# Scales of a two-part kernel: the mask to a power of two moves in front of the step across the partitions, and that step becomes a bfloat16 product instead of a float32 transpose

## The chip, the cores and the metric

The kernel runs on one core of one Trainium2 chip. The metric is the device time of one execution in microseconds. Three runs of the kernel before took 1719.19, 1721.06 and 1722.6 us; the median, 1721.06 us, is the time that a change is measured against. A separate, profiled execution gives the trace.

## The reference

Two independent results stand side by side in the output, 2048 x 2048 in float32.

```python
# A: attention with 32 heads of 32, each position sees itself and the 255 before it
qkv = (x @ wqkv).reshape(B, S, 3, H, Dh).transpose(2, 0, 3, 1, 4)      # S 2048, D 1024
scores = einsum("bhqd,bhkd->bhqk", q, k) * Dh ** -0.5, masked to 0 <= i - j < 256
a = (softmax(scores) @ v).reshape(B, S, D) @ wo
# B: Fourier mixing, real part, by matrices
re, im = einsum("bsd,ed->bse", x, dft_hid_re), einsum("bsd,ed->bse", x, dft_hid_im)
b = einsum("ts,bse->bte", dft_seq_re, re) - einsum("ts,bse->bte", dft_seq_im, im)
return concatenate([a, b], axis=-1)
```

## The kernel before

**Numbers.** Every large product is made from float16 halves. An operand is divided by a power of two s, its value is rounded to float16 (the hi part, on ScalarE), and what is left is rounded to float16 as well (the lo part, on VectorE). A product of two such operands is three float16 products: hi hi, hi lo, lo hi (`PASSES`). The pair of instructions is `split` (L123): an ACTIVATE at L126, then a SCALAR_TENSOR_TENSOR that goes through the helper `vec` and so stands under L120 in the profile.

**Scales.** The power of two of an operand comes from its largest absolute value. Reductions (`top`, or `u_top` on ScalarE) leave the largest of each partition in a tile named `top_...` of 128 x 1 float32 (`spread` joins the pieces). `scale_of` (L158) takes it across the partitions: TensorE transposes the tile, broadcast to 128 x 128, against a float32 identity (`ident`) into a PSUM tile `pt_...`; VectorE reduces that to one maximum on each partition, masks the mantissa away (`bitwise_and` with 0x7F800000, which leaves a power of two), bounds and multiplies it, and takes the reciprocal. 65 scales are made so: 16 for the blocks of the query and key weights (`w_scale`, results in `scw`, and for the input blocks in `vx`), 4 for the blocks of A's input, 2 for the value weights, 1 for the output weights, 8 for B's input (`xp`), 2 for the hidden Fourier matrices (`wd`), and 32 for the column blocks of the sequence Fourier matrices (`u_scale`, results in `sc_u`).

**The start.** Up to the seventh task of the list of projections (`head` and `strict` true) everything is in an order written by hand: `mm` chains each product behind the product before it on TensorE, and `vec` chains each VectorE operation behind the VectorE operation before it. The scale's TensorE step is part of that chain (L161 to L163). The first four projections, one for each of four blocks of query weights, are float32 products of unsplit operands (`d_mm`, tile `pq`, lines L726 to L731), with the scales between them (lines L883 to L918): largest values of weight block 0 and of input block 0, half of the first projection, scale of weight block 0, and so on. Their outputs leave through `qk_out` (tile `yq`, hi on ScalarE at L873, lo on VectorE). Input block 1 is split at L909 to L916, and the float16 projections follow.

**Later.** After the seventh task only TensorE's large products keep their written order. What stands on VectorE, ScalarE and around the scales' TensorE steps is placed by the framework's scheduler, which runs a timeline of its own over the program and gives each engine a fixed queue.

**The Fourier half** runs in four phases of 12 units: four units `x`, in which TensorE makes the hidden transform in blocks (seven products of half size each, `seven`), and eight units `c`, which multiply column blocks of a sequence matrix (`un_a`, `un_b`, `un_c`, split from `raw_u`) by the sums that the units `x` leave in `tsum`, a part of `reg`. The sums are written in `t_fill` (L822: hi on ScalarE at L824, lo on VectorE at L825), the last of them in `t_last`, while the first unit `c` begins: its second product (tile `p_b`) multiplies by a sum whose lo part is the last `reg<-y` of VectorE's fills. Attention of A is woven between the products of both parts (`tick`): scores `s` and `far`, probabilities, their transposed halves, and products `pv`.

Of the kernel before, what the change touches and what calls it, by code (L numbers as in the profile page):

```python
# [9 lines left out]
F32 = mybir.dt.float32  # L10
F32R = mybir.dt.float32r
F16 = mybir.dt.float16
BF16 = mybir.dt.bfloat16
U8 = mybir.dt.uint8
U32 = mybir.dt.uint32
AF = mybir.ActivationFunctionType
ALU = mybir.AluOpType
AX = mybir.AxisListType

P = 128  # L20
# [33 lines left out]
def fused_kernel(ctx: ExitStack, tc: tile.TileContext, xa, wqk, wv, wo, xb, wd, cs, out):  # L54
    nc = tc.nc
# [8 lines left out]
    const = ctx.enter_context(tc.tile_pool(name="const", bufs=1))  # L64
# [13 lines left out]
    tsum = reg1[:, :7 * 8 * CH].rearrange("p (s h k c) -> p s h k c", s=7, h=2, k=4)  # L78
    spare = reg1[:, 7 * 8 * CH:]

    ident = const.tile([P, P], F32, name="ident")
    make_identity(nc, ident)


    upper = const.tile([P, P], F32, name="upper")
# [13 lines left out]
    def bank(name):  # L99
        nbank[0] += 1  # L100
        return ps_m.tile([P, CH], F32, tag=f"m{nbank[0] % 3}", name=name)
# [7 lines left out]
    fixed = []  # L109

    def mm(*args, **kwargs):
        with tc.issue_after(fixed[0].ins) if fixed else nullcontext():
            fixed[:] = [nc.tensor.matmul(*args, **kwargs)]  # L113
        return fixed[0]
# [3 lines left out]
    def vec(f, *args, **kwargs):  # L118
        with tc.issue_after(latest[0].ins) if strict[0] and latest else nullcontext():
            latest[:] = [f(*args, **kwargs)]  # L120
        return latest[0]
# [12 lines left out]
    tops, head = {}, [True]  # L134
# [22 lines left out]

    def scale_of(key, v, s, down=2.0 ** -14):  # L158

        if head[0]:  # L160
            pt = ps_s.tile([P, CH], F32, tag="s", name=f"pt_{key}")[:, :P]  # L161
            with tc.issue_after(fixed[0].ins) if fixed else nullcontext():
                fixed[:] = [nc.tensor.transpose(pt, tops.pop(key).to_broadcast([P, P]), ident)]  # L163
        else:
            pt = (ps_v.tile([P, CH], F32, tag="pv", name=f"pt_{key}") if units_on else bank(f"pt_{key}"))[:, :P]
            nc.tensor.transpose(pt, tops.pop(key).to_broadcast([P, P]), ident)
        vec(nc.vector.tensor_reduce, v, pt, axis=AX.X, op=ALU.max)
        vec(nc.vector.tensor_scalar, v.bitcast(U32), v.bitcast(U32), 0x7F800000, None, op0=ALU.bitwise_and)
        vec(nc.vector.tensor_scalar, v, v, 2.0 ** -100, down, op0=ALU.max, op1=ALU.mult)
        vec(nc.vector.reciprocal, s, v)  # L170

# [245 lines left out]
    def w_scale(kd, g):  # L417
        v = vw[kd, g] = scw[:, "qk".index(kd), g]
        scale_of(f"w{kd}{g}", v[:, 0:1], v[:, 1:2])
# [26 lines left out]
    def x_scale(c):  # L446
        scale_of(f"x{c}", vx[:, 0, c:c + 1], vx[:, 1, c:c + 1])
# [22 lines left out]
    def wv_scale(vh):  # L470
        scale_of(f"wv{vh}", vwv[:, 0, vh:vh + 1], vwv[:, 1, vh:vh + 1])
# [398 lines left out]
    with tc.tile_pool(name="pa", bufs=2) as pa:  # L870
# [49 lines left out]
        for n, (kd, g, c) in enumerate(order):  # L920
# [12 lines left out]
            if kd == "v":  # L933
                t = c
# [9 lines left out]
                                                            op0=ALU.mult, op1=ALU.subtract)]  # L944
# [291 lines left out]
```

## Time and profile before

| | us |
|---|---|
| median of three runs | 1721.06 |
| the profiled execution | 1721.35 |
| its span, first to last instruction | 1719.6 |
| TensorE, products in flight | 1697.2 |
| VectorE busy | 1352.1 |
| ScalarE busy | 1121.0 |
| GpSimd busy | 573.2 |

The trace shows each instruction with its engine (PE is TensorE's products, PEld its weight loads, DVE VectorE, ACT ScalarE, POOL GpSimd, SP the queue that issues most transfers), its line, the tile that it writes and those that it reads, its start and length, and in brackets for how long the engine was idle before it and who ended that. Products are pipelined: one that is listed with 0.27 us holds the queue only until the next one starts, so what a product costs is read from start to start.

### The profile page before, as it was taken

How to read it: one execution, taken by the hardware profiler on the slowest of the kernel's cores; microseconds unless marked ns; L12 is line 12 of the kernel's file. 1: busy time of each engine (PE TensorE's matmuls, PEld its weight loads, DVE VectorE, ACT ScalarE, POOL GpSimd, SP SyncE). 2: the span in 40 equal slices, each digit the busy share in tenths (PEclk: the TensorE clock that was granted, in tenths of full speed). 3: DMA queues.
4: the chain of work that ended last, by engine and by line, in shares of the span. 5: the costliest groups of instructions: out<-in, count | busy, mean ns of one | idle time of the engine just before them, and what ended most of it. 6: DMA issues, size and time to landing. Idle time of an engine off the chain costs nothing.

```text
span 1719.6 us, 30836 instructions
## 1 busy us (share of the span) xinstructions
PE 1697.2 (99%) x10999; PEld 852.5 (50%) x10999; DVE 1352.1 (79%) x2283; ACT 1121.0 (65%) x1939; POOL 573.2 (33%) x874
## 2 busy tenths in 40 slices
PE   9999999999999999999999999999999999999999
PEld 4444555554555544555554555555555545444444
DVE  7878898897998689887688886688886698687542
ACT  3335555576777687888677786678886678563322
POOL 0000332333345341444423464433555424411000
PEclk9999999999999999999999999999999999999999
DMA  9747999999998894887998999986999976875431
GB/s 347 235 140 231 268 287 272 280 255 288 252 230 217 209 234 120 201 195 181 219 259 234 182 185 178 225 208 120 191 183 188 206 197 130 167 188 115 118 98 74
DMA packets 469899, 348.63 MB, mean 203 GB/s; under 512 B 376944, under 2 KB 409968, under 8 KB 468848
## 3 DMA queue, kind: packets, MB, share of 16 engines
q1 hardware_dynamic: 462064, 321.48, 74.2%
q0 software_dynamic: 7680, 25.17, 9.1%
q8 instruction: 86, 1.41, 0.3%
q14 instruction: 69, 0.57, 0.1%
HBM read 166.99 MB, written 106.17 MB: 159 GB/s over the span
## 4 chain that ended last, share of the span: by engine, by line
PE 71%; DVE 11%; DMA 6%; ACT 5%; issue 4%; POOL 2%; SPq 1%; DVEq 0%; ACTq 0%; POOLq 0%
PE p_a L113 19%; PE pv L113 10%; PE p_b L113 9%; PE pk L113 8%; PE pq L113 8%; PE po_a L113 5%; PE p_c L113 5%; DMA raw_u<-in_cs_dram 3%; PE po_b L113 2%; PE s L113 2%; DMA t<-hl 1%; PE po_c L113 1%; PE far L113 1%; DVE reg L825 1%; DVE reg L120 1%
## 5 line engine op out<-in xcount | busy, mean ns | idle before, releaser
L258 ACT ACTIVATE s<-s,bias,escs 128x256 f32<-128x256 f32 (+1 forms) x512 | 270.1, 528 | 11.8
L276 POOL TENSOR_SCALAR_AFFINE_SELECT z<-t 128x512 f16<-128x512 f16 x224 | 182.4, 822 | 175.6 <-PE pv L113 133.4
L251 ACT ACTIVATE bias<-mx,pshift,escs 128x2 f32<-128x2 f32 x256 | 98.2, 384 | 171.5 <-DVE mx L248 171.1
L262 DVE TENSOR_TENSOR hl<-s,hl 128x512 f16<-128x512 f32 (+1 forms) x256 | 169.8, 665 | 48.3 <-ACT hl L261 47.7
L113 PEld LDWEIGHTS <-reg 128*128 128x128 f16 x1344 | 129.0, 98 | 143.2 <-DVE vxp L120 2.0
L278 POOL TENSOR_SCALAR_AFFINE_SELECT t<-t 128x512 f16<-128x512 f16 x224 | 182.8, 825 | 11.4
L113 PE MATMUL p_a<-reg,un_c 128*128 128x512 f16 x768 | 181.2, 379 | 0.2 <-ACT p_c L1057 0.2
L113 PE MATMUL pv<-reg,reg 128*128 128x512 f16 x768 | 173.0, 379 | 1.5 <-DVE vxp L120 1.5
L113 PE MATMUL pk<-reg,wu_k 128*128 128x512 f16 x768 | 174.4, 379 | 0.0
L248 DVE TENSOR_REDUCE mx<-s 128x2 f32<-128x512 f32 (+1 forms) x256 | 171.1, 668 | 3.0
L255 POOL TENSOR_SCALAR mark<-bias 128x1 f32<-128x1 f32 x128 | 53.5, 418 | 353.4 <-ACT bias L251 350.4
L113 PEld LDWEIGHTS <-un_c 128*128 128x128 f16 x1152 | 110.0, 97 | 122.1 <-issue 2.8
L113 PEld LDWEIGHTS <-un_a 128*128 128x128 f16 x1152 | 109.8, 97 | 122.2 <-issue 6.7
L113 PEld LDWEIGHTS <-un_b 128*128 128x128 f16 x1152 | 110.0, 97 | 121.6 <-issue 5.7
L261 ACT ACTIVATE hl<-s 128x512 f16<-128x512 f32 (+1 forms) x256 | 149.0, 582 | 10.6 <-DMA t<-hl 5.1
L113 PE MATMUL pq<-reg,wu_q 128*128 128x512 f16 x672 | 151.3, 379 | 0.8 <-DVE reg L120 0.5
L113 PE MATMUL p_a<-reg,un_a 128*128 128x512 f16 x576 | 136.2, 379 | 4.5 <-DVE y L1025 3.8
L113 PE MATMUL p_b<-reg,un_b 128*128 128x512 f16 x576 | 136.6, 379 | 1.9 <-DVE reg L825 1.9
L113 PE MATMUL p_a<-reg,un_b 128*128 128x512 f16 x576 | 136.4, 379 | 2.1 <-ACT p_c L1057 2.0
L113 PE MATMUL p_c<-reg,un_a 128*128 128x512 f16 x576 | 136.5, 379 | 0.0
L246 DVE COPY_PREDICATED s<-upper,far 128x256 f32<-128x256 uint32 x224 | 94.5, 422 | 43.7 <-PE s L113 42.5
L113 PEld LDWEIGHTS <-qk 96*128 96x128 f16 x1056 | 88.0, 97 | 64.9 <-issue 2.1
(206 smaller groups left out, 3155.7 us busy)
## 6 DMA issues: line engine op xcount, KB each, us to landing
raw_u<-in_cs_dram SPq DMA_DIRECT2D x64, 512.0 KB, 5.0
qk<-qk SPq DMA_DIRECT2D x64, 384.0 KB, 5.2
out_dram<-y POOLq DMA_DIRECT2D x72, 256.0 KB, 6.2
raw_wd<-in_wd_dram SPq DMA_DIRECT2D x24, 512.0 KB, 5.4
vs<-yv SPq DMA_DIRECT2D x32, 264.0 KB, 4.3
vt<-vs SPq DMA_DIRECT2D x64, 132.0 KB, 4.1
raw_wo<-in_wo_dram SPq DMA_DIRECT2D x16, 512.0 KB, 8.4
qk<-yq SPq DMA_DIRECT2D x32, 256.0 KB, 3.6
```

The lines of the kernel that those rows point to most:

```text
L113: fixed[:] = [nc.tensor.matmul(*args, **kwargs)]
L120: latest[:] = [f(*args, **kwargs)]
L246: nc.vector.copy_predicated(s[:, :, P:], upper2, d["far"] if nb == 3 else never2)
L248: nc.vector.tensor_reduce(mx, sv, axis=AX.X, op=ALU.max, negate=True)
L251: nc.scalar.activation(bias, mx, AF.Identity, bias=pshift, scale=es)
L255: marks[:] = [nc.gpsimd.tensor_scalar(mark, bias[:, 0:1], 1.0, None, op0=ALU.mult)]
L258: nc.scalar.activation(sv[:, h], sv[:, h], AF.Exp, bias=bias[:, h:h + 1], scale=es)
L261: nc.scalar.activation(hi, sv, AF.Copy)
L262: behind[:] = [nc.vector.tensor_tensor(lo, sv, hi, op=ALU.subtract)]
L276: nc.gpsimd.affine_select(out=z, in_=pk, compare_op=ALU.is_gt, fill=0.0, base=0, pattern=[[0, 4], [-1, P]], channel_multiplier=1)
L278: nc.gpsimd.affine_select(out=pk, in_=pk, compare_op=ALU.is_ge, fill=0.0, base=0, pattern=[[0, 4], [1, P]], channel_multiplier=-1)
L825: nc.vector.tensor_tensor(lo, src, hi, op=ALU.subtract)
```

## The change

The mask is applied to the `top` tile, before it goes across the partitions, and no longer to the result. The masked float32 is a power of two, so its upper two bytes are the same number in bfloat16. That half, broadcast to 128 x 128, is the stationary operand of an ordinary product with a bfloat16 identity (`unit`); each row of the result is the list of the 128 partitions' powers, and the maximum over it is the power of two of the maximum. The count of operations on VectorE stays. In the start the product goes through `mm`, in the chain, as the transpose did.

```diff
-    ident = const.tile([P, P], F32, name="ident")
-    make_identity(nc, ident)
+    unit = const.tile([P, P], BF16, name="unit")
+    make_identity(nc, unit)
...
     def scale_of(key, v, s, down=2.0 ** -14):
 
+        t = tops.pop(key)
+        vec(nc.vector.tensor_scalar, t.bitcast(U32), t.bitcast(U32), 0x7F800000, None, op0=ALU.bitwise_and)
+        powers = t.bitcast(BF16)[:, 1:2].to_broadcast([P, P])
         if head[0]:
             pt = ps_s.tile([P, CH], F32, tag="s", name=f"pt_{key}")[:, :P]
-            with tc.issue_after(fixed[0].ins) if fixed else nullcontext():
-                fixed[:] = [nc.tensor.transpose(pt, tops.pop(key).to_broadcast([P, P]), ident)]
+            mm(pt, powers, unit, start=True, stop=True)
         else:
             pt = (ps_v.tile([P, CH], F32, tag="pv", name=f"pt_{key}") if units_on else bank(f"pt_{key}"))[:, :P]
-            nc.tensor.transpose(pt, tops.pop(key).to_broadcast([P, P]), ident)
+            nc.tensor.matmul(pt, powers, unit, start=True, stop=True)
         vec(nc.vector.tensor_reduce, v, pt, axis=AX.X, op=ALU.max)
-        vec(nc.vector.tensor_scalar, v.bitcast(U32), v.bitcast(U32), 0x7F800000, None, op0=ALU.bitwise_and)
         vec(nc.vector.tensor_scalar, v, v, 2.0 ** -100, down, op0=ALU.max, op1=ALU.mult)
         vec(nc.vector.reciprocal, s, v)
```

The new function is one line longer, so lines below it are one higher after the change. The scheduler's queues differ in many places. Three of them follow.

VectorE in the start, around the scale of the fourth block of query weights (`top_wq_251` its largest value, `pt_wq_273` the transposed tile, `yq_0_266` the third projection's output). Before:

```order
L120 TENSOR_REDUCE top_wq_251<-raw_wq_141 128x1
L120 TENSOR_REDUCE vx<-pt_x_256 128x1
L120 TENSOR_SCALAR vx<-vx 128x1 x2
L120 RECIPROCAL vx<-vx 128x1
L120 SCALAR_TENSOR_TENSOR reg_83<-raw_x_0_143,vx,reg_83 128x1024
L120 SCALAR_TENSOR_TENSOR reg_83<-raw_x_1_145,vx,reg_83 128x1024
L120 SCALAR_TENSOR_TENSOR yq_0_266<-pq_0_230,f_157,yq_0_266 128x512
L120 TENSOR_REDUCE scw<-pt_wq_273 128x1
```

And now:

```order
L120 TENSOR_REDUCE top_wq_251<-raw_wq_141 128x1
L120 TENSOR_SCALAR top_x_243<-top_x_243 128x1
L120 TENSOR_REDUCE vx<-pt_x_257 128x1
L120 TENSOR_SCALAR vx<-vx 128x1
L120 RECIPROCAL vx<-vx 128x1
L120 SCALAR_TENSOR_TENSOR reg_83<-raw_x_0_143,vx,reg_83 128x1024
L120 SCALAR_TENSOR_TENSOR reg_83<-raw_x_1_145,vx,reg_83 128x1024
L120 SCALAR_TENSOR_TENSOR yq_0_266<-pq_0_230,f_157,yq_0_266 128x512
L120 TENSOR_SCALAR top_wq_251<-top_wq_251 128x1
L120 TENSOR_REDUCE scw<-pt_wq_274 128x1
```

TensorE's transpose needed only the reduction of the first row; its product needs the mask in the last row but one, behind two splits of the input and the third output. In the same stretch ScalarE's half of that output (`yq_0_266`) moves in front of its four splits of the input. Before:

```order
L126 ACTIVATE wu_q_297<-raw_wq_139,scw 128x1024
L126 ACTIVATE reg_83<-raw_x_0_143,vx 128x1024
L126 ACTIVATE reg_83<-raw_x_1_145,vx 128x1024
L126 ACTIVATE reg_83<-raw_x_2_147,vx 128x1024
L126 ACTIVATE reg_83<-raw_x_3_149,vx 128x1024
L873 ACTIVATE yq_0_266<-pq_0_230,f_157 128x512
```

And now:

```order
L126 ACTIVATE wu_q_297<-raw_wq_139,scw 128x1024
L874 ACTIVATE yq_0_266<-pq_0_230,f_157 128x512
L126 ACTIVATE reg_83<-raw_x_0_143,vx 128x1024
L126 ACTIVATE reg_83<-raw_x_1_145,vx 128x1024
L126 ACTIVATE reg_83<-raw_x_2_147,vx 128x1024
L126 ACTIVATE reg_83<-raw_x_3_149,vx 128x1024
```

VectorE at the last of the four phase changes of the Fourier half, some 1418 us into the span before (L825, then L826, are the lo parts of the fills; `un_a` is the first split of the second unit `c`). Before:

```order
L825 TENSOR_TENSOR reg_83<-reg_83 128x512
L246 COPY_PREDICATED s_17855<-upper,far 128x2x128
L825 TENSOR_TENSOR reg_83<-reg_83 128x512
L825 TENSOR_TENSOR reg_83<-y_6773,reg_83 128x512
L248 TENSOR_REDUCE mx_17861<-s_17855 128x2
L782 TENSOR_TENSOR reg_83<-reg_83 128x512
L120 SCALAR_TENSOR_TENSOR un_a<-raw_u_0_17624,sc_u_17831,un_a 128x1024
```

And now:

```order
L826 TENSOR_TENSOR reg_83<-reg_83 128x512
L247 COPY_PREDICATED s_17855<-upper,far 128x2x128
L120 SCALAR_TENSOR_TENSOR un_a<-raw_u_0_17624,sc_u_17831,un_a 128x1024
L249 TENSOR_REDUCE mx_17861<-s_17855 128x2
L826 TENSOR_TENSOR reg_83<-reg_83 128x512
L826 TENSOR_TENSOR reg_83<-y_6773,reg_83 128x512
```

The split `un_a` and the reduction `mx` now stand ahead of the last two fills. ScalarE's half of `un_a` moves in the same way, ahead of the second fill of a pair and of the last one, and so do both halves at the first unit `c` of the three other phases.

## The prediction

> **What bounds the kernel now.** I read the page first, then the transposes by stretch, then the instructions of the first 60 us on TensorE (PE), VectorE (DVE) and ScalarE (ACT), then the four places where the Fourier half changes phase. Three rows of the page:
>
> ```profile
> PE 1697.2 (99%) x10999; PEld 852.5 (50%) x10999; DVE 1352.1 (79%) x2283; ACT 1121.0 (65%) x1939; POOL 573.2 (33%) x874
> ...
> PEclk9999999999999999999999999999999999999999
> ...
> PE 71%; DVE 11%; DMA 6%; ACT 5%; issue 4%; POOL 2%; SPq 1%; DVEq 0%; ACTq 0%; POOLq 0%
> ```
>
> TensorE has work in flight 99% of the span at an undiminished clock, and it holds 71% of the chain that ended last. So two things count: time taken from TensorE's queue, and time for which that queue has to stand. VectorE at 79% matters where TensorE waits for it.
>
> The transposes, as the windows of one line (L166; six more, of line L163, stand in the first 32 us):
>
> ```profile
> 0.00:60.00 60.00, 0.32 (x1) 0.13 (x1) 1.00 0.87 317
> 60.00:1720.00 1660.00, 15.97 (x58) 7.92 (x58) 1.00 0.84 199
> ```
>
> 58 of the 65 scales are made after the first 60 us, seven in it. The start, on TensorE (start, length, count):
>
> ```profile
> 1.25 4.45 PE L711 MATMUL wps<-reg 128*128 128x512 f16 x10 [1.25 <-DVE reg L703]
> ...
> 9.89 0.27 PE L163 MATMUL pt_wq<-ident,top_wq 128*128 128x128 f32 x1
> ...
> 22.24 0.27 PE L163 MATMUL pt_wq<-ident,top_wq 128*128 128x128 f32 x1
> 22.35 7.03 PE L113 MATMUL pq<-wx,raw_wq 128*128 128x512 f32 x16
> ...
> 31.05 0.27 PE L163 MATMUL pt_wq<-ident,top_wq 128*128 128x128 f32 x1
> 31.16 3.60 PE L113 MATMUL pq<-wx,raw_wq 128*128 128x512 f32 x8
> 34.59 2.97 PE L113 MATMUL pq<-reg,wu_q 128*128 128x512 f16 x13
> 38.06 12.89 PE L113 MATMUL pq<-reg,wu_q 128*128 128x512 f16 x59 [0.50 <-DVE reg L120]
> 51.28 0.32 PE L166 MATMUL pt_x<-ident,top_x 128*128 128x128 f32 x1 [0.33 <-DVE top_x L120]
> 51.92 8.36 PE L113 MATMUL pq<-reg,wu_q 128*128 128x512 f16 x38 [0.33 <-DVE yq L120]
> ```
>
> None of the first transposes is waited for: TensorE gets to them without a pause, since their input (one reduction) is long there. What it does wait for are three small things at 38.06, 51.28 and 51.92.
>
> **Part 1, the product in place of the transpose.** From 22.24 to 22.35 a transpose holds the queue for 0.11 us. The nearest rows for a two-byte product of 128 columns, each with its own weight load, are two score products:
>
> ```profile
> 918.30 0.22 PE L113 MATMUL far<-qk,qk 96*128 96x128 f16 x1
> 918.36 0.22 PE L113 MATMUL s<-qk,qk 96*128 96x128 f16 x1
> ```
>
> One start to the next is 0.06 us (0.055 before rounding, 128 columns at the 0.43 ns that a 512-column product's 0.22 us gives per column). So a scale saves 0.055 us of TensorE, and 58 of them 58 x 0.055 = 3.2 us; the other seven are in part 2. From both sides: if loading a broadcast weight shows on the queue, the product may cost the 0.11 us of before and the saving is 0; no row has 128 columns in under 0.055 us, so 3.2 is also the most. I take 3.2, by the nearest row, since 918.30 and 918.36 are weight load and product in just this pattern.
> [...]
>
> **Part 2, the mask in front of the product, in the first 40 us.** The mask (a TENSOR_SCALAR on 128x1) was done after the transpose; now TensorE's product waits for it. In this stretch VectorE takes its work strictly in the order of the program, and the mask is issued where the scale is asked for, behind everything that VectorE was given since the reduction. VectorE there:
>
> ```profile
> 11.10 0.28 DVE L120 TENSOR_REDUCE scw<-pt_wq 128x1 f32<-128x128 f32 x1
> 11.42 0.34 DVE L120 TENSOR_SCALAR scw<-scw 128x1 uint32<-128x1 uint32 x2
> ...
> 14.60 0.29 DVE L120 TENSOR_REDUCE vx<-pt_x 128x1 f32<-128x128 f32 x1 [1.46 <-PE pt_x L163]
> ...
> 23.52 0.75 DVE L120 SCALAR_TENSOR_TENSOR yq<-pq,f,yq 128x512 f16<-128x512 f32 x1 [0.82 <-ACT yq L873]
> 24.18 0.28 DVE L120 TENSOR_REDUCE scw<-pt_wq 128x1 f32<-128x128 f32 x1
> ...
> 29.53 0.29 DVE L120 TENSOR_REDUCE vx<-pt_x 128x1 f32<-128x128 f32 x1 [0.81 <-PE pt_x L163]
> ...
> 31.61 2.48 DVE L120 SCALAR_TENSOR_TENSOR reg<-raw_x,vx,reg 128x1024 f16<-128x1024 f32 x2 [1.22 <-ACT reg L126]
> 35.30 0.75 DVE L120 SCALAR_TENSOR_TENSOR yq<-pq,f,yq 128x512 f16<-128x512 f32 x1 [1.21 <-ACT yq L873]
> 35.96 0.28 DVE L120 TENSOR_REDUCE scw<-pt_wq 128x1 f32<-128x128 f32 x1
> ```
>
> A mask costs 0.17 us (two small operations in 0.34), and TensorE starts about 0.06 us after the VectorE operation that it waits for (the pair in part 3). Of the seven scales here three find TensorE early:
> - First weight block. The mask comes where the reduction at 11.10 stood: 11.10 + 0.17 + 0.06 = 11.33. TensorE was there at 9.89: a wait of 1.4 us, with all float32 products of the queue behind it. VectorE's next two reductions of a pt were waiting for TensorE anyway (the 1.46 at 14.60), so they come 1.3 us later, and, with one operation fewer behind the product, VectorE runs 1.1 us late.
> - Third weight block. The mask now stands behind yq of 23.52, as 24.18 did: 23.52 + 1.1 + 0.66 = 25.28, and with 0.17 and 0.06 the product starts at 25.51. TensorE comes at 22.24 + 1.3 = 23.5: a wait of 2.0 us; it is now 3.3 late.
> - Fourth weight block, the dearest. The reduction at 29.53 waits for TensorE, so it and the two splits of 31.61 come 3.0 later, at 34.6, and end 2.4 later at 37.0. The yq of 35.30 follows at once: its 1.21 us of waiting goes, because ScalarE now has its half of that output ahead of four splits. ScalarE before:
>
> ```profile
> 30.42 4.26 ACT L126 ACTIVATE reg<-raw_x,vx 128x1024 f16<-128x1024 f32 x4 [4.20 <-DVE vx L120]
> 34.60 0.67 ACT L873 ACTIVATE yq<-pq,f 128x512 f16<-128x512 f32 x1
> ```
>
>   Then the mask: 37.0 + 0.66 + 0.17, and 0.06, gives 37.9. TensorE comes at 31.05 + 3.2 = 34.2: a wait of 3.7 us.
>
> TensorE is then 6.8 us late, and starts the float16 products at 41.4, not 34.59. VectorE is only some 2 us late by then (the reduction of 35.96 comes at 38.2), so the three old waits are over when TensorE gets there. They were, by starts, with 0.217 us a product ((2.97 - 2.32) / 3, of 13 here and 10 in part 3): 34.59 + 13 x 0.217 = 37.41 against 38.06, 0.65; 38.06 + 59 x 0.217 = 50.86 against 51.28, 0.4; 51.28 + 0.11 against 51.92, 0.5. That repays 1.6. What is left is **5.2 us**, carried on, because from here on VectorE's next splits wait for scales and outputs that TensorE has yet to make.
>
> Past 60 us the mask costs nothing: it is ready several us before TensorE is at the product (the schedule is no longer strict, and moves the product back where the mask is late), and VectorE's count is unchanged.
>
> **Part 3, the order at four phase changes.** With one small operation fewer behind the product, the scheduler places the first split of the next column block (un_a) earlier on both engines. At the first block of each Fourier phase it now stands ahead of the last fills (reg<-reg, reg<-y) of the sum that TensorE multiplies by. The last of the four places, on TensorE, VectorE and ScalarE, in before:
>
> ```profile
> 1417.61 2.32 PE L113 MATMUL p_b<-reg,un_b 128*128 128x512 f16 x10
> 1420.41 0.59 PE L113 MATMUL p_b<-reg,un_b 128*128 128x512 f16 x2 [0.48 <-DVE reg L825]
> ```
>
> ```profile
> 1419.67 0.68 DVE L825 TENSOR_TENSOR reg<-y,reg 128x512 f16<-128x512 f32 x1
> 1420.27 0.68 DVE L248 TENSOR_REDUCE mx<-s 128x2 f32<-128x512 f32 x1
> ...
> 1421.47 1.28 DVE L120 SCALAR_TENSOR_TENSOR un_a<-raw_u,sc_u,un_a 128x1024 f16<-128x1024 f32 x1
> ```
>
> ```profile
> 1417.48 1.14 ACT L824 ACTIVATE reg<-reg 128x512 f16<-128x512 f32 x2
> ...
> 1419.04 1.13 ACT L126 ACTIVATE un_a<-raw_u,sc_u 128x1024 f16<-128x1024 f32 x1
> ```
>
> The eleventh product needs the last reg<-y (below: the last fill), which ends at 1419.67 + 0.68 = 1420.35; TensorE goes on 0.06 later. Now ScalarE's un_a takes the second half's place of the pair at 1417.48: it ends at 1418.05 + 1.13 = 1419.2. VectorE's un_a waits for that; un_a, mx, a fill and the last fill then take 1.2 + 0.6 + 0.6 + 0.68 (each start to start, 0.08 less than its length, the last in full): 1422.3. TensorE's wait grows by **1.9 us**. At the three other places only un_a comes before the fills. They are:
>
> ```profile
> 660.50 1.02 PE L113 MATMUL p_b<-reg,un_b 128*128 128x512 f16 x4
> ...
> 915.28 0.59 PE L113 MATMUL p_b<-reg,un_b 128*128 128x512 f16 x2 [1.06 <-DVE reg L825]
> ...
> 1165.52 0.59 PE L113 MATMUL p_b<-reg,un_b 128*128 128x512 f16 x2 [0.33 <-DVE reg L825]
> ```
>
> ```profile
> 660.01 0.69 DVE L825 TENSOR_TENSOR reg<-y,reg 128x512 f16<-128x512 f32 x1
> ```
>
> At 915.28 and 1165.52 TensorE waits already, so each grows by 1.2. At 660.50 it doesn't: the eleventh product starts at 660.50 + 2 x 0.217 = 660.93, the fill ends at 660.70, so 0.2 is spare and 1.0 is paid. Together 1.9 + 1.2 + 1.2 + 1.0 = **5.3 us**. The lower bound is 0, if other VectorE work of the same stretch slips behind instead; the upper is some 7, if ScalarE's own delay of 1.1 adds at two more places.
>
> **The sum.** 5.2 + 5.3 - 3.2 = +7.3 us on the profiled execution's 1721.35 us (span 1719.6 and 1.75 around it). That execution lies 0.3 over the median of 1721.06, against which the result will stand: 1721.06 + 7.3 = 1728.4 us, 0.42% slower. About 0.2%, 3.4 us, is what a measurement of this kernel can tell from no change.
>
> **The rivals.**
> - Head only: the four phase changes cost nothing. For it: VectorE's total is the same and it has 21% idle. Against: the order puts a 1.28 us pass ahead of an operation for which TensorE already waits. 5.2 - 3.2 = +2.0, 1723.1, within 0.2%. Chance 0.14.
> - The other side: the delays are repaid. TensorE's later waits would end at times set by VectorE, ScalarE and SyncE alone, so a TensorE that comes late finds them over; the place is every wait past 60 us, the price all that parts 2 and 3 add. Only the saving stays, 65 x 0.055 = 3.6: 1717.5. For it: waits such as the three at 38 to 52 us are repaid in just this way. Against: VectorE's reductions at 14.60 and 29.53 wait for TensorE, so the queues move together. It decides for faster only if all but 0.1 of the 10.5 us comes back. Chance 0.05, and of that 0.03 over the 0.2%.
> - The clock. The rows above show it at half rate once: ten warm-up products in 4.45 us, 0.43 each against 0.217 later. The longest pause in the head would be the 3.7 us at 34.2. If a pause of this length brings half rate back for as long as that row, half of 4.45 is lost, 2.2 us: 1730.6. Against: no pause lowers PEclk in the page's row, though the waits quoted are at most 1.1 us. Chance 0.08.
>   [...]
> - The product is no cheaper than the transpose, its weight load showing: 3.2 more, 1731.6. Chance 0.05.
>
> **How the numbers follow.** Forecast 0.68, rivals 0.14, 0.05, 0.08 and 0.05. Its own range is 1725.7 (half of part 3) to 1731.7 (part 3 at its upper bound, 1.7 more, and half the saving gone). To hold eight in ten with the unknown bounds: from 1722.5, which takes in head only, to 1733.0, which takes in the clock and a dear product. Slower over 0.2%: 0.66 of the forecast's 0.68, the clock and the dear product, 0.79; faster 0.03; the rest, 0.18, within.
>
> **What would show it.** On TensorE in the changed profile: waits of about 1.4, 2.0 and 3.7 us for a masked top before 40 us, float16 products from about 41 us, none of the waits of 38 to 52 us; pt products 0.055 us apart from what follows; at the first block of each phase a wait for the last fill of 2 us or so, with un_a before it on VectorE. Wrong would be: float16 products that start before 38 us, or a last fill that ends as early after the phase change as before, or a span under 1721.

## The result and the profile after

The changed kernel took 1735.58 us (median of 4 runs, 1728.48 to 1739.85) beside 1721.83 us for the kernel before on the same chip (4 runs, 1719.19 to 1725.03). The measured ratio is 1.0064, with an interval of 1.0036 to 1.0092: slower, by less than 1%. (It is not the quotient of the two medians, which is 1.0080 and lies in the same interval.) On a second chip it was 1.0058 (1.0033 to 1.0082). The direction was forecast. By the ratio the change costs 11.0 us, which is 1732.1 us on the 1721.06 that the forecast was made against: 3.7 us above the forecast of 1728.4 and inside the range, near its upper end of 1733.0. The median of 1735.6 itself lies 2.6 us above that end, so the range held only narrowly. The profiled execution, 1728.48 us with a span of 1726.8, happens to be the fastest of the four and lands on the forecast; that is luck in good part, as will be seen. Two runs of the experiments lie far outside all others, at 6335 and 2270 us, and count in no ratio.

TensorE (PE) in the first 62 us of the changed kernel (start, length, what ran, and in brackets the idle time ahead of it and what ended that):

```profile
11.51 0.23 PE L113 MATMUL pt_wq<-unit,top_wq 128*128 128x128 bf16 x1 [1.60 <-DVE top_wq L120]
...
15.93 0.22 PE L113 MATMUL pt_x<-unit,top_x 128*128 128x128 bf16 x1
15.98 1.94 PE L113 MATMUL pq<-wx,raw_wq 128*128 128x512 f32 x4
...
25.77 0.23 PE L113 MATMUL pt_wq<-unit,top_wq 128*128 128x128 bf16 x1 [1.74 <-DVE top_wq L120]
...
38.17 0.29 PE L113 MATMUL pt_wq<-unit,top_wq 128*128 128x128 bf16 x1 [3.42 <-DVE top_wq L120]
38.26 6.63 PE L113 MATMUL pq<-wx,raw_wq 128*128 128x512 f32 x8
44.73 16.57 PE L113 MATMUL pq<-reg,wu_q 128*128 128x512 f16 x76
61.13 0.22 PE L168 MATMUL pt_x<-unit,top_x 128*128 128x128 bf16 x1
```

The three waits for a masked top are there, at 11.5, 25.8 and 38.2 us, and the float16 products run from 44.73 without the three old waits. VectorE (DVE) shows why the third is so long: the largest value of the fourth weight block is there at 30.40 us, its mask comes at 37.97.

```profile
29.19 1.21 DVE L120 TENSOR_REDUCE top_wq<-raw_wq 128x1 f32<-128x1024 f32 x1
...
37.97 0.14 DVE L120 TENSOR_SCALAR top_wq<-top_wq 128x1 uint32<-128x1 uint32 x1
```

What was not in the sum is the row of 38.26: eight float32 products in 6.63 us, where before needed 3.60. The windows of the changed kernel say why (busy times of the engines, then the granted clock, then the DMAs):

```profile
30.00:40.00 10.00, 6.58 (x15) 2.60 (x14) 5.70 (x13) 5.74 (x6) 0.00 (x0) 0.87 0.59 191
40.00:50.00 10.00, 10.00 (x32) 4.21 (x31) 7.23 (x9) 1.05 (x2) 0.00 (x0) 0.79 0.87 285
```

The granted clock is 0.87 and 0.79, where before had 1.00: behind its longest wait TensorE ran at half rate for a few microseconds (the clock is 0.50 from 38 to 44 us and 1.00 from 45 to 60).

The phase changes, on TensorE, with the waits for the last fills:

```profile
667.57 0.59 PE L113 MATMUL p_b<-reg,un_b 128*128 128x512 f16 x2 [1.74 <-DVE reg L826]
```

```profile
920.86 0.38 PE L113 MATMUL p_b<-reg,un_b 128*128 128x512 f16 x1 [0.28 <-ACT reg L825]
923.00 0.59 PE L113 MATMUL p_b<-reg,un_b 128*128 128x512 f16 x2 [1.77 <-DVE reg L826]
```

```profile
1171.06 0.38 PE L113 MATMUL p_b<-reg,un_b 128*128 128x512 f16 x1 [0.51 <-ACT reg L825]
1172.55 0.59 PE L113 MATMUL p_b<-reg,un_b 128*128 128x512 f16 x2 [1.11 <-DVE reg L826]
```

```profile
1424.72 0.38 PE L113 MATMUL p_b<-reg,un_b 128*128 128x512 f16 x1 [0.51 <-ACT reg L825]
1426.80 1.01 PE L113 MATMUL p_b<-reg,un_b 128*128 128x512 f16 x2 [1.71 <-DVE reg L826]
```

And what VectorE does ahead of the last of them:

```profile
1423.66 1.28 DVE L120 SCALAR_TENSOR_TENSOR un_a<-raw_u,sc_u,un_a 128x1024 f16<-128x1024 f32 x1
1424.86 0.68 DVE L249 TENSOR_REDUCE mx<-s 128x2 f32<-128x512 f32 x1
1425.46 0.68 DVE L826 TENSOR_TENSOR reg<-reg 128x512 f16<-128x512 f32 x1
1426.06 0.69 DVE L826 TENSOR_TENSOR reg<-y,reg 128x512 f16<-128x512 f32 x1
```

un_a, mx, a fill and the last fill, in the order that the prediction gave. Idle time before these products was 0, 1.06, 0.33 and 0.48 us before the change, and is 1.74, 2.05, 1.62 and 2.22 now (both rows of a place added): 5.8 us more.

A useful mark for how much of the head is left later is the start of the first pt_xp, which no row of the head overlaps. The view of that one tile gives it for before and then for the changed kernel (duration least, median, most; first and last start):

```profile
L166 PE MATMUL pt_xp<-ident,top_xp x1: 272/272/272, 128.3 to 128.3; 128*128 128x128 f32 x1
```

```profile
L168 PE MATMUL pt_xp<-unit,top_xp x1: 219/219/219, 137.0 to 137.0; 128*128 128x128 bf16 x1
```

The head costs 137.0 - 128.3 = 8.7 us. It is called the mark below.

### The profile page after: what moved, and what is told of

Its sections match the earlier page's. It is cut to its first block, busy times and chain, and to the rows that moved or that the text cites. A ratio compares the mean times of both kernels' runs of the same rounds, so it can differ in the third digit from the quotient of the medians.

```text
span 1726.8 us, 30830 instructions
## 1 busy us (share of the span) xinstructions
PE 1697.6 (98%) x10999; PEld 849.1 (49%) x10999; DVE 1351.5 (78%) x2283; ACT 1118.5 (65%) x1939; POOL 576.5 (33%) x874
## 4 chain that ended last, share of the span: by engine, by line
PE 75%; DVE 10%; ACT 6%; DMA 4%; issue 4%; POOL 1%; SPq 0%; DVEq 0%; POOLq 0%; ACTq 0%
PE p_a L113 21%; PE p_b L113 11%; PE pv L113 10%; PE pk L113 7%; PE pq L113 7%; PE p_c L113 6%; PE po_a L113 5%; PE po_b L113 2%; PE s L113 2%; DVE reg L826 1%; PE po_c L113 1%; PE far L113 1%; DMA t<-hl 1%; DVE mx L249 1%; DVE hl L263 1%
## 5 line engine op out<-in xcount | busy, mean ns | idle before, releaser
L279 POOL TENSOR_SCALAR_AFFINE_SELECT t<-t 128x512 f16<-128x512 f16 x224 | 185.4, 834 | 11.5
```

The lines of the kernel that those rows point to most:

```text
L279: nc.gpsimd.affine_select(out=pk, in_=pk, compare_op=ALU.is_ge, fill=0.0, base=0, pattern=[[0, 4], [1, P]], channel_multiplier=-1)
```

## The experiments

The scatter of single runs is some 5 us either way on the chips of the experiments, so an interval is about 0.2% wide to each side with twelve runs. The marks and waits come from one profile each and repeat much better: the seven profiles below and above whose head has no late mask and no added products (before, late, first_old, early, both, both_again, late_tail) have the mark between 127.7 and 128.5 us.

**The mask behind the product again (late).**

```diff
         t = tops.pop(key)
-        vec(nc.vector.tensor_scalar, t.bitcast(U32), t.bitcast(U32), 0x7F800000, None, op0=ALU.bitwise_and)
...
         vec(nc.vector.tensor_reduce, v, pt, axis=AX.X, op=ALU.max)
+        vec(nc.vector.tensor_scalar, v.bitcast(U32), v.bitcast(U32), 0x7F800000, None, op0=ALU.bitwise_and)
```

> The bfloat16 product stays, but the mask goes back behind it, onto the maximum that the product has carried over (the upper half of a float32 keeps its exponent, so the scale is the same number). Theory: the slowdown comes whole from where the mask stands (the waits of the head, and the order that one operation fewer behind the product gives at the phase changes), and the product itself saves 65 x 0.055 = 3.6 us: 1721.8 - 3.6 = 1718.2 us, ratio 0.998, no wait for a masked top before 40 us, un_a again behind the last fills. Rival, a product no cheaper or a saving that later waits take back: ratio 1.000, 1721.8. Rival, something else of the product (its weight load of a broadcast column, bfloat16 between float16 products) costs: ratio about 1.004 and more, as with the whole change.

Measured: 1723.69 us beside 1724.74, ratio 0.9988 (0.9969 to 1.0008); the mark is at 128.2 us, no wait for a masked top in the head, float16 products from 34.76. Its waits for the last fills are those of before (1.9 us in three). So the bfloat16 product as such costs at most 1.4 us, where the whole change costs 10 to 11; the slowdown comes with the place of the mask. Whether the product's whole 3.6 us are saved this run cannot say: the interval reaches from -5.3 to +1.4 us.

**The first six scales back in the old form (head_old).** The transpose's identity stands in the memory of `upper` until that is needed.

```diff
...
-        vec(nc.vector.tensor_scalar, t.bitcast(U32), t.bitcast(U32), 0x7F800000, None, op0=ALU.bitwise_and)
+        if not head[0]:
+            vec(nc.vector.tensor_scalar, t.bitcast(U32), t.bitcast(U32), 0x7F800000, None, op0=ALU.bitwise_and)
...
-            mm(pt, powers, unit, start=True, stop=True)
+            with tc.issue_after(fixed[0].ins) if fixed else nullcontext():
+                fixed[:] = [nc.tensor.transpose(pt, t.to_broadcast([P, P]), upper)]
...
+        if head[0]:
+            vec(nc.vector.tensor_scalar, v.bitcast(U32), v.bitcast(U32), 0x7F800000, None, op0=ALU.bitwise_and)
...
```

> The first seven scales (those of the first 40 us) go back to the float32 transpose with the mask behind it; all later scales keep the changed form. Theory: the head's 5.2 us and the slow clock behind its last wait (3.0 us in the changed profile) vanish, the four phase changes stay: - 3.2 + 5.3 to 7.7 = +2.1 to +4.5 us on before, 1724 to 1726, ratio 1.001 to 1.003; float16 products start at 34.6, waits of about 1.9 us at 1420 and 915 stay. Rival, head only (the phase changes cost nothing that later work doesn't repay): -3.2, 1718.6, ratio 0.998. Rival, the excess of the medians over the profiled run (7 us) has nothing to do with the head: 1731 and more, ratio 1.006.

Measured: 1737.56 us, ratio 1.0072 (1.0038 to 1.0106), as slow as the whole change. The expectation failed. The head is as before up to 52 us, and then TensorE of this kernel shows two new waits:

```profile
52.05 5.34 PE L111 MATMUL pq<-reg,wu_q 128*128 128x512 f16 x24 [0.97 <-DVE yq L118]
57.23 0.22 PE L168 MATMUL pt_x<-unit,top_x 128*128 128x128 bf16 x1
59.40 0.38 PE L111 MATMUL pq<-reg,wu_q 128*128 128x512 f16 x1 [1.95 <-ACT reg L124]
62.31 3.94 PE L111 MATMUL pq<-reg,wu_q 128*128 128x512 f16 x11 [2.53 <-DVE reg L118]
```

The seventh scale (the expectation counted it to the head, but the head's form ends with the sixth), pt_x of the third block of x, has its place chosen by the scheduler. With a mask in front it puts this product behind 96 float16 products, where before had it behind 72, so one whole output, 24 products of 0.217 us, goes ahead of it. VectorE then gets that scale at 57.49, not 53.58, and TensorE stands for the splits: 1.95 and 2.53 us, and the clock falls again (0.72 in the window 60 to 66 us). The mark is at 134.9, 6.6 us late. In the changed kernel itself the delay (there 76 float16 products) is hidden, since TensorE comes 10 us late anyway. So a cost stood behind the head's cost, and undoing the first alone only uncovers it. With the phase changes' 5.8 us and the product's saving this makes some 9 us of the measured 12.4 (6.6 to 18.3); the profile has another wait of 4.8 us, for z at 1503 us, which before has not and which is not explained here.

**The first eight scales in the old form (first_old).** As before, with the blocks of x and of the first weights taken by name, so that the seventh and eighth go back too; pt_x then stands behind 72 float16 products again. (The two expectations below that speak of 76 and 100 count the four float32 products ahead of them too; the profile lists those as eight.)

```diff
...
+        old = key[:2] in ("wq", "x0", "x1", "x2", "x3") and nold[0] < 9
+        nold[0] += 1
+        if not old:
             vec(nc.vector.tensor_scalar, t.bitcast(U32), t.bitcast(U32), 0x7F800000, None, op0=ALU.bitwise_and)
...
```

> The eight scales of the first 75 us (four weight blocks, four blocks of x) in the old form, a float32 transpose with the mask behind it; the other 57 in the changed form. Unlike the run that put back only the first six, it has pt_x of the third block of x behind 76 products again, not 100. Theory: the head is as before (first pt_xp at 128 us), and what is left is - 57 x 0.055 = - 3.1, and 6.4 at the phase changes: +3.3 us, up to +4.6, ratio 1.0019 to 1.0027, the same as with the early mask. Rival, the phase changes cost nothing: ratio 0.998. Rival, the run before it stayed slow for another reason than pt_x's place: first pt_xp at 134 us or later and ratio 1.005 or more.

Measured: 1727.2 us beside 1723.31, ratio 1.0012 (0.9993 to 1.0032), mark at 128.5. The interval holds the theory's 1.0019 to 1.0027 for the phase changes alone, and neither rival (0.998, and 1.005 or more). The mark settles the point on pt_x.

**The early mask (early).** The same mask, given out right behind the reduction, in `spread`.

```diff
         tops[key] = t1
+        vec(nc.vector.tensor_scalar, t1.bitcast(U32), t1.bitcast(U32), 0x7F800000, None, op0=ALU.bitwise_and)
...
         t = tops.pop(key)
-        vec(nc.vector.tensor_scalar, t.bitcast(U32), t.bitcast(U32), 0x7F800000, None, op0=ALU.bitwise_and)
```

> The changed kernel with the mask given out right behind the reduction that makes the largest value, not where the scale is asked for; VectorE has the same operations. Theory: no product of the head finds its mask late, so the head is as before (no wait for a masked top, pt_x again behind 76 products, the first pt_xp at about 128 us as in before, not 137), while the order at the four phase changes stays that of the changed kernel: - 3.6 + 6.4 (the four longer waits of the changed profile) = +2.8 us, up to +4.1 with a half-rate stretch behind the last, ratio 1.0016 to 1.0024. Rival, the phase changes cost nothing in the end: ratio 0.998. Rival, the mask in front costs wherever it stands: the first pt_xp stays beyond 134 us, ratio 1.005 and more.

Measured: 1728.45 us, ratio 1.0021 (1.0001 to 1.0041), mark at 128.2, as the theory had it; both rivals lie outside the interval. TensorE in its head:

```profile
9.79 0.22 PE L113 MATMUL pt_wq<-unit,top_wq 128*128 128x128 bf16 x1
...
22.14 0.22 PE L113 MATMUL pt_wq<-unit,top_wq 128*128 128x128 bf16 x1
...
30.94 0.22 PE L113 MATMUL pt_wq<-unit,top_wq 128*128 128x128 bf16 x1
31.00 3.65 PE L113 MATMUL pq<-wx,raw_wq 128*128 128x512 f32 x8
34.49 15.93 PE L113 MATMUL pq<-reg,wu_q 128*128 128x512 f16 x72
```

No product waits, and the eight float32 products take 3.65 us. A mask in front of the product costs the head nothing if it is given out early; what cost was its place in VectorE's strict order. It also parts the two causes: the order at the phase changes goes with the one operation fewer behind the product, which this kernel has and the late form has not, and not with a late mask. The waits for the last fills are those of the changed kernel, and are what this kernel has left (TensorE's waits, by what is waited for: us in total, times, longest):

```profile
PE p_b L113 <- DVE reg L826: 6.3, 4, 1.8
...
PE p_b L113 <- ACT reg L825: 1.3, 3, 0.5
```

**un_a held back at the phase changes (tail, and again for its profile, tail_again).** The split of each phase's second column block is tied behind the last fill.

```diff
+    filled = []
+
     def t_fill(k, i, src, n=2):
...
-        nc.scalar.activation(hi, src, AF.Copy)
-        nc.vector.tensor_tensor(lo, src, hi, op=ALU.subtract)
+        filled[:] = [nc.scalar.activation(hi, src, AF.Copy),
+                     nc.vector.tensor_tensor(lo, src, hi, op=ALU.subtract)]
...
-            t = pair("a", r1)
+            with ExitStack() as held_up:
+                if kind == "c" and i == 1:
+                    for f in filled:
+                        held_up.enter_context(tc.issue_after(f.ins))
+                t = pair("a", r1)
```

> The changed kernel, with un_a of the second column block of each phase held back on VectorE and ScalarE until the last fill of the sum is given out. Theory: the waits of 1.90, 1.93, 1.27 and 1.87 us at 668, 923, 1173 and 1427 shrink to before's 0, 1.2, 0.5 and 0.6 or below, and the half rate behind the last of them goes: 5.3 to 7.7 us less than the changed kernel, 1728 to 1730 by its median, ratio to before about 1.002 to 1.004. The head is untouched: float16 products still from 44.7 us in the profile. Rival, the waits at the phase changes are not due to that order (or un_a, now later, is waited for itself): no faster than the changed kernel, ratio 1.006.

> The changed kernel with un_a of each phase's second column block held back behind the last fill, for its profile. Theory: the waits at the phase changes shrink to 1.2, 0.5 and 0.6 us or less and the first one goes, the head keeps its 8.7 us (first pt_xp at 137), so 5.3 to 7.7 us under the changed kernel: ratio to before 1.002 to 1.0045. Rival, holding back un_a makes TensorE wait for it instead: no gain, ratio as the changed kernel.

Measured: 1730.16 us over eleven runs, ratio 1.0035 (1.0012 to 1.0057), and on the second try 1730.12 beside 1723.88, ratio 1.0037 (1.0020 to 1.0054). The waits of the second try's profile:

```profile
PE pt_wq L113 <- DVE top_wq L120: 6.9, 3, 3.4
...
PE p_b L113 <- DVE reg L832: 1.3, 2, 1.0
```

The waits for fills went from 6.3 and 1.3 us to 1.3 and none, while the head's 6.9 us stayed (the mark is at 135.6: the clock behind the 3.42 us pause cost 1.3 us less than in the changed kernel, 5.32 us for the eight products and not 6.63). At the last place no wait was left because TensorE came late: half rate, behind a wait of 1.04 us for y, had cost it 1.5 us there (seven products in 3.15 us, where 1.67 would do). The rival, that un_a would be waited for instead, is out: no wait of TensorE for un_a is listed. Beside the changed kernel measured with it on the same chip (1.0058) this is 0.21% less, some 3.6 us, which the two intervals alone do not set apart from nothing (0.3% either way); between the early mask alone and with this edit (below, both runs) it is 0.38%, 6.6 us, and that is clear (0.24% either way).

**A filled pause (fillp).** 50 products that nothing reads go to TensorE ahead of the product of the fourth weight block.

```diff
...
+            for k in range(50 if key == "wq3" else 0):
+                mm(pt[:, P:2 * P], unit, unit, start=True, stop=True)
...
```

> The changed kernel, with 50 products of unit with unit (128 columns each, 50 x 0.055 = 2.75 us, into a part of the bank that nothing reads) given to TensorE ahead of the product of the fourth weight block: TensorE then stands for 0.8 us at 38 us instead of 3.6, and nothing else moves. Theory, the clock: the eight float32 products behind the pause run at full rate again (3.6 us for eight instead of 6.63), float16 products start at 41.7 instead of 44.73, the granted clock of 30 to 50 us is 1.00, and the time falls by 3.0 us on the changed kernel. Rival, the eight products were slow for another reason (their operands, a queue): 44.7 as before, no gain. Second rival, half rate comes back by TensorE's load over a longer stretch and not by this pause: it shows later, and the gain is below 1 us.

TensorE in this kernel:

```profile
34.62 2.96 PE L113 MATMUL pt_wq<-unit 128*128 128x128 bf16 x50
38.20 0.23 PE L113 MATMUL pt_wq<-unit,top_wq 128*128 128x128 bf16 x1 [0.63 <-DVE top_wq L120]
38.27 3.65 PE L113 MATMUL pq<-wx,raw_wq 128*128 128x512 f32 x8
41.76 16.78 PE L113 MATMUL pq<-reg,wu_q 128*128 128x512 f16 x77
```

```profile
30.00:40.00 10.00, 9.37 (x67) 1.00 0.62 211
40.00:50.00 10.00, 10.00 (x44) 1.00 0.96 317
```

The product comes at 38.20 as in the changed kernel (38.17), but the clock stays at 1.00, the eight float32 products take 3.65 us, and the float16 products start at 41.76 instead of 44.73: 3.0 us, as the theory had it. The mark is at 134.0, not 137.0. So of the head's 8.7 us 3.0 are the clock and 5.7 the waits. The same pause of 3.42 us cost less in two other profiles, those of the repeat of the changed kernel and of un_a held back, 5.35 and 5.32 us for the eight products, 1.7 us more than 3.65:

```profile
39.92 0.23 PE L113 MATMUL pt_wq<-unit,top_wq 128*128 128x128 bf16 x1 [3.42 <-DVE top_wq L120]
39.98 5.35 PE L113 MATMUL pq<-wx,raw_wq 128*128 128x512 f32 x8
```

```profile
38.17 0.29 PE L113 MATMUL pt_wq<-unit,top_wq 128*128 128x128 bf16 x1 [3.42 <-DVE top_wq L120]
38.26 5.32 PE L113 MATMUL pq<-wx,raw_wq 128*128 128x512 f32 x8
```

The time as a whole, 1737.55 us and ratio 1.0078 (1.0051 to 1.0104) over six runs, shows no gain; its own profile has a wait of 3.8 us for a qk load at 423 us (1.5 in before), and a mean granted clock of 0.998, with 1.00 in its first 70 us. The 3.0 us at the mark are shown, a gain at the end is not.

**Early mask and held-back un_a together (both, and again, both_again).**

> The early mask, and un_a of each phase's second column block held back behind the last fill. Theory: both causes of the slowdown are gone and the product's saving stays, 65 x 0.055 = 3.6 us; before's own waits at the phase changes (1.2, 0.5, 0.6 us) go as well: -3.6 to -5.9 us, ratio 0.9966 to 0.998; the first pt_xp at 128 us. Rival, waits take the saving back (the later ones end at times that VectorE, ScalarE and SyncE set): ratio 1.000. Rival, a third cause in the change that neither edit removes: above 1.001.

> The early mask and the held-back un_a together, once more, since the first interval (0.9960 to 1.0003) just holds no change. Theory: the product's 3.6 us of TensorE stay saved, in part or whole: ratio 0.9966 to 0.9985. Rival: the later waits take it back as they took back some 9 of the 26 us that 472 added products held the queue for: ratio 0.999 to 1.000.

Measured: 1720.95 us beside 1723.31, ratio 0.9981 (0.9960 to 1.0003), and 1721.09 beside 1725.91, ratio 0.9984 (0.9966 to 1.0003). Weighted by their widths the two give 0.9983 (0.9969 to 0.9997), 2.9 us faster than before and the lowest ratio here, though the late form's 0.9988 is not set apart from it. The last phase change in it, TensorE and VectorE:

```profile
1418.26 0.59 PE L113 MATMUL p_b<-reg,un_b 128*128 128x512 f16 x2 [0.48 <-DVE reg L832]
```

```profile
1417.52 0.68 DVE L832 TENSOR_TENSOR reg<-y,reg 128x512 f16<-128x512 f32 x1
1418.12 0.68 DVE L249 TENSOR_REDUCE mx<-s 128x2 f32<-128x512 f32 x1
```

The wait is before's own 0.48 us, and the mark is at 127.8. TensorE's listed waits sum to 18.0 us, in before to 17.9. That before's own waits for the fills would go as well, the further part of the theory, did not come true (1.8 us here, 1.9 in before). No third cause is left that this resolution could see.

**The late mask and held-back un_a (late_tail).** Both edits from above on one kernel.

> The bfloat16 product with the mask behind it, and un_a of each phase's second column block held back behind the last fill. Theory: - 3.6 us from the product, and before's waits at the phase changes (1.2, 0.5, 0.6 us) gone, -3.6 to -5.9 us, ratio 0.9966 to 0.998, the same as early mask and held-back un_a together, since where the mask stands costs nothing if neither the head nor the order waits for it. Rival, VectorE's un_a, now later, is waited for itself: no better than the product with the mask behind it alone, ratio 0.999.

Measured: 1722.37 us, ratio 1.0006 (0.9984 to 1.0028). The theory's 0.9966 to 0.998 lies outside the interval, so this expectation failed; the rival's 0.999 lies in it. But what the rival rests on isn't there: no wait of TensorE for un_a is listed, and the waits for the last fills are before's 1.9 us. The late form had the order of before already, so the edit had nothing to take away. Its profiled execution (1732.64 us, the slowest of the twelve) shows stalls of 3.4 us for a load at 1337, which no other profile has, and 2.6 us for z at 1496, which the late form has too. Why this kernel isn't as fast as the early mask with un_a held back stays open; the two intervals overlap.

**Nine products for one (nine).** On the late form; each scale outside the head repeats its product, and the last writes what the others wrote.

```diff
...
-            nc.tensor.matmul(pt, powers, unit, start=True, stop=True)
+            for k in range(9):
+                nc.tensor.matmul(pt, powers, unit, start=True, stop=True)
...
```

> The kernel with the mask behind the product, each of the 59 scales outside the head now with nine products of the same operands in place of one (the last writes what the others wrote): 472 more, one after the other. It measures the price of one. At 0.055 us, as the single ones stand in the profiles: +26 us on the single ones, 1748, ratio to before 1.014. [...] At the 0.11 us of the transpose: +52 us, ratio 1.029.

Measured: 1739.04 us beside 1723.88, ratio 1.0093 (1.0064 to 1.0123): 16.0 us on before (11.0 to 21.2). Neither of the two times expected (ratios of 1.014 and 1.029) came. A piece of its TensorE queue:

```profile
708.19 0.67 PE L168 MATMUL pt_u<-unit,top_u 128*128 128x128 bf16 x9
708.69 0.22 PE L113 MATMUL far<-qk 96*128 96x128 f16 x1
```

Nine take 0.50 us from start to start, 0.055 each, weight load and all. So the price is the first of the two, and the dearer one is out; the times were wrong since they took each microsecond of the queue as paid. 472 products hold the queue for 26 us, and with the 3.6 us that the 65 scales save it is 22.4 us longer than before's. Some 70% of that was paid (by the interval half to nearly all). The profiles show where most of the rest went: TensorE's listed waits sum to 13.8 us, in before to 17.9.

## Why the prediction was right and wrong

The direction and both mechanisms were right, and both were sized well. What was mis-sized is the clock, which stood among the rivals and belonged in the sum: 3.0 us in the head and 1.6 us at the last phase change. The repayment by later waits, put at 0.05 as a whole, came in part and hid it. By its steps:

- **Part 1, the product.** 0.055 us from one start to the next, as said (15.93 to 15.98 in the changed kernel, and nine in 0.50 us). What the saving is worth at the end is less sure than the 3.2 us of the sum: the best form is 2.9 us faster (0.5 to 5.3), the nine products were paid by some 70%.
- **Part 2, the head.** Waits of 1.4, 2.0 and 3.7 us were predicted, 1.60, 1.74 and 3.42 came, at 11.51, 25.77 and 38.17 us instead of 11.33, 25.51 and 37.9; the old waits of 38 to 52 us went. The 5.2 us carried on measure 5.7, once the clock is taken out. The early mask shows the cause: with the same operations given out earlier, all of it goes.
- **"Past 60 us the mask costs nothing."** This step stopped too late and looked at the wrong thing. The seventh scale (51 us) has its product moved back by the scheduler, and with a punctual TensorE that costs 6.6 us at the mark. It cost nothing here only because the head's delay covered it. That the product is moved back where the mask is late was written down as a harmless fact; who waits for that product's scale was not asked.
- **Part 3, the phase changes.** 1.9, 1.2, 1.2 and 1.0 us were predicted, in the order 1420, 915, 1165 and 660; the growth was 1.7, 1.0, 1.3 and 1.7, together 5.8 instead of 5.3. Holding back un_a removes it, and 3.6 or 6.6 us of time with it, by two comparisons of which only the second is clear of the scatter.
- **The clock, the failed size.** It stood as a rival with a chance of 0.08 and one price of 2.2 us, sized from the warm-up row (the granted clock is listed as 1.00 there; only the length of the products, 0.43 us against 0.217, says half rate). It came true: 3.0, 1.7 and 1.7 us behind the 3.42 us pause in the three profiles that have it, and then again elsewhere. The last phase change of the changed kernel is followed by another 1.6 us: the two products of 1426.80 take 0.81 us from start to start instead of 0.43, the granted clock is 0.50 from 1426.8 to 1430 us, and eleven float16 products take 3.75 us in the row below, where 2.32 + 0.22 would do (the ten of before's 1417.61 and one more):

```profile
1427.61 3.75 PE L113 MATMUL p_a<-reg,un_c 128*128 128x512 f16 x11
```

  In the repeat on the second chip the granted clock is below 1.00 in five windows: 0.89 from 5 to 20 us, 0.91 from 30 to 50 and from 415 to 435, 0.83 from 920 to 930 and from 1420 to 1430. Three of these stretches stand behind waits that the change adds; those after 415 and after 1420 us stand behind waits for a load and for y that before has too, though shorter. The repeat's mark, 137.4, fits: two stretches of 1.7 us in its head, behind the first and the third wait, stand in place of the one of 3.0. The windows of 920 to 930 and 1420 to 1430 us of the profiled execution, and the first of them of the repeat:

```profile
920.00:930.00 10.00, 7.96 (x41) 1.00 0.67 252
1420.00:1430.00 10.00, 7.78 (x31) 0.83 0.07 27
```

```profile
920.00:930.00 10.00, 7.96 (x34) 0.83 0.70 265
```

  The mean granted clock over all runs was 0.9961 for the changed kernel (11 runs) and 0.9993 for before (the 18 beside its repeat); 0.0032 of 1730 us is 5.5 us, an upper estimate, since the mean counts idle time too (in the changed kernel's profile the clock is 0.85 from 36 to 38 us, where no product runs). Within each kernel the longer runs are those with the lower clock (correlations from -0.5 to -0.9). So a wait of a microsecond or two that the change adds can have half rate behind it: of the waits for a mask or a last fill in the changed kernel's profile, those of 3.42 and 1.71 us have it, and those of 1.60, 1.74 (twice), 1.77 and 1.11 us have not. It is not the whole of the scatter: the four runs of the changed kernel have mean clocks of 0.996 or 0.997, a difference of some 2 us by these figures, so why three of them took 7 to 11 us longer than the profiled one stays open.
- **"The delays are repaid."** In part: 8.7 us at the mark are 6.4 us at the first pt_u (635.3 and 641.7 us), where the product's saving on the 22 scales between explains 1.2; the listed waits of that stretch shrink by only 0.2 us, and what made the rest is not shown. More comes back later: TensorE's waits for y and p_c sum to 7.7 us in before and to 4.2 us here. Over the whole span its listed waits grow from 17.9 to 24.6 us, 6.7 us, although the head and the phase changes add 12.5. With 4.6 us of the clock and 3.6 saved by the product this gives 7.7 us, where the spans differ by 7.2. So the profiled execution ends at the forecast because two things that the sum did not have, the clock and most of this repayment, nearly cancel: that is luck.

Set against each other, the head costs 0.37 to 0.53% (the repeat of the changed kernel against the early mask alone, and un_a held back without and with the early mask), the phase changes 0.21 to 0.38%, and the rest gains 0.17%. Each of these differences is uncertain by 0.2 to 0.3% to each side; they agree with one another, and no smaller effect is separated.

## What to carry to other kernels

When a small operation is moved from behind a product to in front of it, look at where the instruction stands in its engine's queue, not at its 0.15 us: the fourth weight block's reduction was done at 30.4 us and its mask came at 38.0, since it stood behind another scale, two splits and an output. Give such an operation out where its input is made. When one piece of a change is undone and the time doesn't move, look for the next wait behind it before the theory is dropped, and carry a stage's end (here the first pt_xp) as a mark, which one profile settles where a dozen timed runs do not.

## What the runs showed of the hardware

- Half rate of TensorE's clock follows pauses much shorter than the 3.42 us that had it in the changed kernel. At the second phase change a pause of 1.77 us left the clock at 1.00 in one execution, and in another, the repeat, a pause of 1.76 us was followed by half rate (0.83 in the window above): the first six products take 2.40 us, where six took 1.46 shortly before. With un_a held back, waits of 0.91 and 1.04 us with one short product between them were followed by it too: seven products in 3.15 us, where 1.67 would do. The pause of 0.63 us behind the filler products was not.

```profile
923.52 0.59 PE L113 MATMUL p_b<-reg,un_b 128*128 128x512 f16 x2 [1.76 <-DVE reg L826]
923.95 2.40 PE L113 MATMUL p_a<-reg,un_c 128*128 128x512 f16 x6
```

  Which pause is followed by it differs from one execution to the next, so it acts like a scatter. That this grows with the waits alone is not shown: the kernel with both edits has the waits of before, and a mean clock of 0.9983 beside 0.9993. What decides it no run here shows.
- What a half-rate stretch costs varies too: behind the same 3.42 us pause 3.0, 1.7 and 1.7 us in three executions, and 1.6 us behind the 1.71 us pause at the last phase change.
- A bfloat16 product whose weights are one column broadcast to 128 costs no more than a float16 score product: 0.05 to 0.06 us from start to start singly, and 0.50 us for nine in a row, 0.055 each.
